# Weight chunks in the order a, a, b, b for the first FFN step, and the last store from another queue

## The chip, the cores and the metric

One core of a Trainium2 chip. The metric is device time in microseconds (us) of one execution; lower is better. Faster or slower needs 2%.

## The reference

A linear attention with decay (4 batches, 8 heads, 768 positions, head size 64) feeds a bilinear FFN on 3072 tokens:

```python
def _attn_ref(q, k, v, lam):            # blocks of 64 positions, cut
    for b in range(nb):
        intra = (qb kb^T * Dmask) vb
        inter = (qb * lam_pow) kv_state
        out = intra + inter
        kv_state = lam_block * kv_state + (kb * rev_pow)^T vb

def _moe_ref(x, w_a, w_b, w_out):       # 512 -> 1536 -> 512
    a = x @ w_a
    b = x @ w_b
    return (a * b @ w_out).astype(np.float32)
```

## The kernel before

The kernel works on 24 blocks of 128 tokens, in groups; TensorE (PE) runs the FFN of one group with the attention of later blocks woven in at "slots". What matters here is the first group, in which the weights are still arriving, and the store of the last rows. SyncE (SP) issues the loads in the order of `pending`; each of the six chunks of `w_a` and of `w_b` (512 KB) is cast to bf16 before use.

```python
W_CHUNKS = (256,) * 6
...
    a_pool = ctx.enter_context(tc.tile_pool(name="a", bufs=3))
...
    pending = []
    for c in range(len(W_CHUNKS)):
        pending += [("a", c), ("b", c)]
...
    def prep_v(u):                       # v of block u to bf16
        make_vb(u, "pool" if u < n0 + 3 else "dve")       # n0 = 4
        pump()
...
    def kv_copy(u, ps, eng="dve"):       # the running state, PSUM to SBUF
        ...
            nc.vector.tensor_mul(st..., ps..., bdiag_bc)
...
    def a_part(f, xT, gt, cuts=None):    # 4 matmuls of 512 columns, copy on ACT
        ps = half(wa_sb, f, xT, gt, "a_ps", cuts)
        a_sb = a_pool.tile([128, 512], BF16, name="a_sb", tag="a")
        nc.scalar.copy(a_sb[:, :gt], ps[:, :gt])
        return a_sb

    def b_part(f, xT, gt, a_sb, ab):     # 4 matmuls, product on DVE
        ps = half(wb_sb, f, xT, gt, "b_ps")
        nc.vector.tensor_mul(ab[:, f, :gt], a_sb[:, :gt], ps[:, :gt])
...
    def store(row, op, lo, hi):
        ...
        o_sb = o_pool.tile([128, d_model], F32, name="o_sb", tag="osb")
        nc.scalar.copy(o_sb[:, lo:hi], op[:, lo:hi])
        nc.sync.dma_start(out=out_r[row][:, lo:hi], in_=o_sb[:, lo:hi])
...
    # ffn(), first group; each chunk holds two f
            for c, w in enumerate(W_CHUNKS):
                fs = range(w_off[c] // 128, w_off[c + 1] // 128)
                a_sbs = [a_part(...) for f in fs]
                if c + 1 < len(W_CHUNKS):
                    cast_w("a", c + 1, "dve")
                for f, a_sb in zip(fs, a_sbs):
                    b_part(f, xT, gt, a_sb, ab)
                    hook(f)              # slot 0: state matmuls of block 3
                if c + 1 < len(W_CHUNKS):
                    cast_w("b", c + 1, "act")
...
    cast_w("a", 0, "pool")               # two instructions of half a chunk
    cast_w("b", 0, "dve")
```

Of the kernel before, what the change touches and what calls it, by code (L numbers as in the profile page):

```python
# [26 lines left out]

GROUPS = (4, 1, 2, 4, 4, 4, 4, 1)
W_CHUNKS = (256,) * 6
W_BUFS = 12  # L30
LOOKAHEAD = (3, 2)
DMA_T_FROM = 9
# [32 lines left out]
def kernel(  # L65
# [11 lines left out]
    nc = tc.nc  # L77
# [4 lines left out]
    d_model, d_ff = moe_w_a.shape  # L82
# [7 lines left out]
    singles = ctx.enter_context(tc.tile_pool(name="singles", bufs=1))  # L90
    wst_pool = ctx.enter_context(tc.tile_pool(name="wst", bufs=W_BUFS))
    ld_pool = ctx.enter_context(tc.tile_pool(name="ld", bufs=4))
# [1 line left out]
    qkT_pool = ctx.enter_context(tc.tile_pool(name="qkT", bufs=5))  # L94
    msk_pool = ctx.enter_context(tc.tile_pool(name="msk", bufs=4))
    xT_pool = ctx.enter_context(tc.tile_pool(name="xT", bufs=2))
    a_pool = ctx.enter_context(tc.tile_pool(name="a", bufs=3))
    ab_pool = ctx.enter_context(tc.tile_pool(name="ab", bufs=2))
    o_pool = ctx.enter_context(tc.tile_pool(name="o", bufs=4))
    ps_pool = ctx.enter_context(tc.tile_pool(name="ps", bufs=1, space=PSUM))  # L100
# [7 lines left out]
    def ps_bank(name, shape, dt, hold=False, ffn=False, at=None):  # L108
        i = bank["next"] if at is None else at
        while i in bank["held"] or (ffn and i == bank["ffn"]):  # L110
            i = (i + 1) % 7
        if ffn:
            bank["ffn"] = i
        bank["next"] = (i + 1) % 7
        if hold:
            bank["held"].add(i)
        return ps_pool.tile(shape, dt, name=name, tag=f"ps{i}")
# [19 lines left out]
    staged = {}  # L137
    w_off = [sum(W_CHUNKS[:i]) for i in range(len(W_CHUNKS) + 1)]

    def load_w(kind, c):  # L140
# [4 lines left out]
        else:  # L145
            w = W_CHUNKS[c]
            t = t[:, :KS * w].rearrange("p (k n) -> p k n", k=KS)
# [4 lines left out]
    def cast_w(kind, c, eng):  # L152
        t = staged.pop((kind, c))
        if kind == "o":
            dst = wo_sb[:, 2 * c:2 * c + 2, :]
        else:
            dst = (wa_sb if kind == "a" else wb_sb)[:, :, w_off[c]:w_off[c + 1]]
        if eng == "act":
            nc.scalar.copy(dst, t)  # L159
        elif eng == "pool":  # L160
            nc.gpsimd.tensor_copy(dst[:, :, :128], t[:, :, :128])
            nc.gpsimd.tensor_copy(dst[:, :, 128:], t[:, :, 128:])
        else:
            nc.vector.tensor_copy(dst, t)  # L164
        pump()

    pending = []
    for c in range(len(W_CHUNKS)):
        pending += [("a", c), ("b", c)]
    n0 = GROUPS[0]  # L170
    pending += [("o", c) for c in range(4)] + [("q", n0), ("k", n0)]
    pending += [("o", 4), ("o", 5), ("v", n0)]
# [4 lines left out]
    def pump():  # L177
        while pending:
            kind, c = pending[0]
            if kind in "abo":  # L180
                if len(staged) >= W_BUFS:
                    return
            elif c >= used["u"] + LOOKAHEAD[used["u"] > 9]:
                return
            pending.pop(0)
            if kind in "abo":
                load_w(kind, c)
            else:
                load_x(kind, c)
# [15 lines left out]
    for w, src in (("q", q), ("k", k)):  # L205
        x4_r = src[0, :, 0:PACK * BLK, :].rearrange("h (p r) d -> p h (r d)", r=PACK)
        for h in range(0, H, 2):
            t = ld_pool.tile([128, H * D], F32, name=w + "4", tag=w + "f")
# [219 lines left out]
    out_r = out.rearrange("(t p) n -> t p n", p=128)  # L428
# [10 lines left out]
    def a_part(f, xT, gt, cuts=None):  # L439
# [5 lines that stand above are left out]
    def b_part(f, xT, gt, a_sb, ab):  # L445
        ps = half(wb_sb, f, xT, gt, "b_ps")
        nc.vector.tensor_mul(ab[:, f, :gt], a_sb[:, :gt], ps[:, :gt])  # L447
# [4 lines left out]
        row, o_sb = kept.pop(0)  # L452
        nc.sync.dma_start(out=out_r[row], in_=o_sb)

    def store(row, op, lo, hi):
        if row < g_u0[KEEP_GROUPS]:
            o_sb = wst_pool.tile([128, 1024], F32, name="o_kept", tag="wst")[:, :d_model]
            nc.scalar.copy(o_sb, op)  # L458
            kept.append((row, o_sb))
            return  # L460
        o_sb = o_pool.tile([128, d_model], F32, name="o_sb", tag="osb")
        nc.scalar.copy(o_sb[:, lo:hi], op[:, lo:hi])  # L462
        nc.sync.dma_start(out=out_r[row][:, lo:hi], in_=o_sb[:, lo:hi])

    def out_mms(op, ab, t, fs, lo=0, hi=d_model):
        for f in fs:
            nc.tensor.matmul(op[:, lo:hi], lhsT=ab[:, f, t * 128:(t + 1) * 128],  # L467
                             rhs=wo_sb[:, f, lo:hi], start=(f == 0), stop=(f == FC - 1))

    def ffn(u0, n, xT, hook, first, last):  # L470
        gt = n * BLK
        ab = ab_pool.tile([128, FC, 512], BF16, name="ab", tag="ab")
        if first:
            for c, w in enumerate(W_CHUNKS):
                fs = range(w_off[c] // 128, w_off[c + 1] // 128)
                a_sbs = [a_part(f, xT, gt, ((0, gt - BLK), (gt - BLK, gt)) if f == 0 else None)
                         for f in fs]
                if c + 1 < len(W_CHUNKS):
                    cast_w("a", c + 1, "dve")
                for f, a_sb in zip(fs, a_sbs):  # L480
                    b_part(f, xT, gt, a_sb, ab)
                    hook(f)
                if c + 1 < len(W_CHUNKS):
                    cast_w("b", c + 1, "act")
            ops = [ps_bank("op", [128, d_model], F32, hold=True) for _ in range(n)]
            slot = FC
            for c in range(FC // 2):
                for t in range(n):
                    out_mms(ops[t], ab, t, range(2 * c, 2 * c + 2))
                    if c == FC // 2 - 1:  # L490
                        store(u0 + t, ops[t], 0, d_model)
                    hook(slot)
                    slot += 1
            bank["held"].clear()
            return
        for f in range(FC):
            a_sb = a_part(f, xT, gt)
            b_part(f, xT, gt, a_sb, ab)
            hook(f)
        for t in range(n):  # L500
            op = ps_bank("op", [128, d_model], F32, ffn=True)
            if last and t == n - 1:
                for lo, hi in ((0, 256), (256, 384), (384, 512)):
                    if lo:
                        op = ps_bank("op", [128, d_model], F32, ffn=True)
                    out_mms(op, ab, t, range(FC), lo, hi)
                    store(u0 + t, op, lo, hi)
                return
            out_mms(op, ab, t, range(FC // 2))
            hook(FC + 2 * t)  # L510
            out_mms(op, ab, t, range(FC // 2, FC))
            store(u0 + t, op, 0, d_model)
            hook(FC + 2 * t + 1)
# [124 lines left out]
    natural_k((3,), (0, 1, 2, 3), 3)  # L638
    cast_w("a", 0, "pool")
    bank["held"].clear()  # L640
    cast_w("b", 0, "dve")
    used["u"] = n0
    pump()

    for g, n in enumerate(GROUPS):
# [6 lines left out]
        def hook(slot, plan=plan):  # L652
            for name, us in plan.get(slot, ()):
                if name == "C":
                    cast_w("o", us, "dve")
                elif name == "PK":
                    prep_k(us)
                elif name == "PV":
                    prep_v(us)
                elif name == "P":  # L660
                    prep_k(us)
                    prep_v(us)
                elif name == "W":
                    store_kept()
                elif name == "T":
                    piece_T(us)
                elif name == "S":
                    piece_S(us)
                elif name == "V":
                    piece_V(us)  # L670
                elif name == "O":
                    pieces_O((us,))
                elif name == "O2":
                    pieces_O(us)
                else:
                    pieces_O(us[:2], us[2:])

        ffn(g_u0[g], n, gx.pop(g), hook, g == 0, g + 1 == len(GROUPS))

# [28 lines left out]
```

## Time and profile before

| | before |
|---|---|
| time, median of 3 | 233.59 us (233.25 to 234.13) |
| span of the profiled execution | 232.6 us |
| PE waits for a weight in the first group | 0.8 us, once |
| first a-matmul of the first chunk / of the third a-chunk | 18.16 / 26.40 us |
| end of the last copy / end of the span | 229.68 / 232.6 us |

The time of a run is some 1.7 us above its span. The profiled execution itself took 234.34 us. PE is busy nearly all the time, so the table names the only two places that the change touches: the first group's weights, and what comes after the last matmul.

### The profile page before, as it was taken

The page shows a single profiled execution, that of the slowest core. Times are in us where ns is not written, and L with a number is a line of the kernel's source. Part 1 is how long each engine was busy: PE and PEld are TensorE (multiplying, and loading weights), DVE is VectorE, ACT ScalarE, POOL GpSimd, SP SyncE. Part 2 cuts the span into 40 slices and gives each one's busy share as a digit, 9 for nine tenths or more (in the row PEclk, how much of TensorE's full clock was granted, in tenths as well). Part 3 has the DMA queues.
Part 4 walks back from the last instruction along what each step waited for, and adds up shares of the span by engine and source line. Part 5 has one row for each costly group of instructions (what it writes and reads, how often), then busy time and mean ns, then how long its engine had stood idle before and what let it go on. Part 6 is the DMA issues. An engine that isn't in the chain of part 4 may idle for free.

```text
span 232.6 us, 4506 instructions
## 1 busy us (share of the span) xinstructions
PE 223.8 (96%) x1756; PEld 124.8 (54%) x1779; DVE 116.4 (50%) x204; ACT 91.0 (39%) x172; POOL 50.4 (22%) x65
## 2 busy tenths in 40 slices
PE   7798999999999999999999999999999999999994
PEld 2574444449698654454544454544454544444493
DVE  1894666646479745684335474235483323332050
ACT  3683764056564342332233332333332333332261
POOL 6061000245655243333300543000300000000000
PEclk9999999999999999999999999999999999999999
DMA  4999999999999999999959997229300220000311
GB/s 150 300 264 351 348 361 298 268 209 193 204 223 164 214 188 221 217 171 205 333 192 206 213 181 129 93 92 202 69 3 0 90 93 0 1 0 10 128 45 48
DMA packets 96453, 38.84 MB, mean 167 GB/s; under 512 B 83376, under 2 KB 91952, under 8 KB 96432
## 3 DMA queue, kind: packets, MB, share of 16 engines
q1 hardware_dynamic: 96288, 38.54, 72.8%
q8 instruction: 14, 0.23, 0.4%
q14 instruction: 7, 0.06, 0.1%
q10 hardware_dynamic: 144, 0.00, 0.0%
HBM read 28.32 MB, written 6.29 MB: 149 GB/s over the span
## 4 chain that ended last, share of the span: by engine, by line
PE 87%; DMA 6%; SPq 3%; ACT 1%; issue 1%; DVE 0%
PE a_ps L434 26%; PE b_ps L434 26%; PE op L467 26%; DMA wst<-in_moe_w_a_dram 4%; SPq L128 3%; PE kq L308 2%; PE o_ps L350 2%; DMA q<-in_q_dram 2%; PE o_ps L340 2%; PE kvd L364 1%; PE tps L294 1%; SPq L149 1%; ACT o_kept L458 1%; DVE wa_sb L164 0%; PE kvd L385 0%
## 5 line engine op out<-in xcount | busy, mean ns | idle before, releaser
L447 DVE TENSOR_TENSOR ab<-a_sb,b_ps 128x512 bf16<-128x512 bf16 (+2 forms) x96 | 52.5, 552 | 76.7 <-PE b_ps L434 55.2
L434 PE MATMUL a_ps<-xT,wa_sb 128*128 128x512 bf16 (+3 forms) x378 | 76.5, 323 | 1.7 <-DVE wa_sb L164 0.8
L434 PE MATMUL b_ps<-xT,wb_sb 128*128 128x512 bf16 (+2 forms) x383 | 77.0, 326 | 0.1
L442 ACT CAST a_sb<-a_ps 128x512 bf16<-128x512 f32 (+2 forms) x96 | 45.5, 481 | 61.5 <-PE a_ps L434 58.1
L467 PE MATMUL op<-wo_sb,ab 128*128 128x512 bf16 (+2 forms) x300 | 64.2, 362 | 0.8 <-issue 0.3
L434 PEld LDWEIGHTS <-wb_sb 128*128 128x128 bf16 x384 | 34.4, 98 | 28.9 <-ACT wb_sb L159 0.5
L434 PEld LDWEIGHTS <-wa_sb 128*128 128x128 bf16 x388 | 33.9, 98 | 29.6 <-DVE wa_sb L164 1.3
L467 PEld LDWEIGHTS <-ab 128*128 128x128 bf16 x312 | 28.8, 98 | 29.9
L325 DVE TENSOR_TENSOR m<-kq,lotri 128x512 bf16<-128x512 f32 x47 | 29.3, 682 | 17.2 <-PE kq L308 17.1
L257 POOL TENSOR_TENSOR qk<-kf,lp_k 128x512 bf16<-128x512 f32 x18 | 19.0, 1056 | 75.1 <-PE a_ps L434 38.1
L262 POOL TENSOR_TENSOR qk<-qf,lp_q 128x512 bf16<-128x512 f32 x20 | 21.8, 1092 | 24.1 <-DMA qf<-in_q_dram 24.1
L462 ACT COPY o_sb<-op 128x512 f32<-128x512 f32 (+2 forms) x19 | 10.3, 541 | 34.0 <-PE op L467 34.0
L357 ACT CAST xT<-o_ps 128x512 bf16<-128x512 f32 x22 | 12.0, 590 | 18.1 <-PE o_ps L350 17.5
L396 DVE TENSOR_TENSOR st<-kvd,bdiag 128x512 bf16<-128x512 f32 x18 | 12.3, 683 | 3.9 <-PE kvd L364 3.2
L271 DVE CAST vb<-vf 128x512 bf16<-128x512 f32 x17 | 9.5, 560 | 0.0
L296 ACT COPY qkT<-tps 128x1024 bf16<-128x1024 bf16 x5 | 5.1, 1012 | 9.9 <-PE tps L294 9.9
L197 PE MATMUL idle<-idle_sb 128*128 128x128 bf16 (+1 forms) x31 | 7.1, 371 | 1.3 <-DVE idle_sb L192 1.3
L350 PE MATMUL o_ps<-m,vb 128*64 128x128 bf16 x192 | 7.9, 222 | 0.0
L271 POOL CAST vb<-vf 128x512 bf16<-128x512 f32 x7 | 4.4, 631 | 13.6 <-DMA vf<-in_v_dram 13.6
L159 ACT CAST wb_sb<-wst 128x1024 bf16<-128x1024 f32 x5 | 5.2, 1046 | 4.7 <-DMA wst<-in_moe_w_b_dram 4.7
L340 PEld LDWEIGHTS <-st 128*128 128x128 bf16 x80 | 5.4, 98 | 2.8
L308 PE MATMUL kq<-qkT 64*128 64x128 bf16 x160 | 6.6, 218 | 0.0
(57 smaller groups left out, 87.4 us busy)
## 6 DMA issues: line engine op xcount, KB each, us to landing
vf<-in_v_dram SPq DMA_DIRECT2D x24, 256.0 KB, 4.9
qf<-in_q_dram SPq DMA_DIRECT2D x20, 256.0 KB, 4.6
kf<-in_k_dram SPq DMA_DIRECT2D x20, 256.0 KB, 4.7
out_dram<-o_sb SPq DMA_DIRECT2D x16, 256.0 KB, 2.0
wst<-in_moe_w_a_dram SPq DMA_DIRECT2D x6, 512.0 KB, 8.8
wst<-in_moe_w_b_dram SPq DMA_DIRECT2D x6, 512.0 KB, 8.8
wst<-in_moe_w_out_dram SPq DMA_DIRECT2D x6, 512.0 KB, 8.6
out_dram<-o_kept SPq DMA_DIRECT2D x7, 256.0 KB, 2.8
```

Source lines behind the costliest of these rows:

```text
L257: eng_of(eng).tensor_mul(qk[:, 1], raw.pop((u, "k")), lp_k[:, u % NB].to_broadcast([128, H, D]))
L262: eng_of(eng).tensor_mul(U[u]["qk"][:, 0], raw.pop((u, "q")), lp_q[:, u % NB].to_broadcast([128, H, D]))
L271: eng_of(eng).tensor_copy(vb, vf)
L308: nc.tensor.matmul(kq[i][:, hp, :], lhsT=d["kT"][p, hp, :], rhs=d["qT"][p, hp, :], start=True, stop=True, skip_group_check=True)
L325: nc.vector.tensor_mul(m, kq[i], lotri_bc)
L350: nc.tensor.matmul(d["o"][p, hp, :], lhsT=d["vb"][:, 2 * hp + i, :], rhs=d["m"](i, hp), start=(first and hp == 0), stop=True, skip_group_c ...
L357: nc.scalar.copy(xT[:, :, col:col + BLK], o_ps)
L396: nc.vector.tensor_mul(st[:].rearrange("p hp i d -> p hp (i d)"), ps[:].rearrange("p hp i d -> p hp (i d)"), bdiag_bc)
L434: nc.tensor.matmul(ps[:, lo:hi], lhsT=w_sb[:, s, f * 128:(f + 1) * 128], rhs=xT[:, s, lo:hi], start=(s == 0), stop=(s == KS - 1), skip_gro ...
L442: nc.scalar.copy(a_sb[:, :gt], ps[:, :gt])
L447: nc.vector.tensor_mul(ab[:, f, :gt], a_sb[:, :gt], ps[:, :gt])
L467: nc.tensor.matmul(op[:, lo:hi], lhsT=ab[:, f, t * 128:(t + 1) * 128], rhs=wo_sb[:, f, lo:hi], start=(f == 0), stop=(f == FC - 1))
```

## The change

The intent: PE does the four a-parts of the first two chunks before it needs any b-weight, so that it has work while b0 travels; and the last store leaves from the queue of the engine that made its data. The diff, less hunks that only carry arguments:

```diff
+W_STEPS = ((0, 1), (2,), (3,), (4,), (5,))
-    a_pool = ctx.enter_context(tc.tile_pool(name="a", bufs=3))
+    a_pool = ctx.enter_context(tc.tile_pool(name="a", bufs=5))
-    for c in range(len(W_CHUNKS)):
-        pending += [("a", c), ("b", c)]
+    for cs in W_STEPS:
+        pending += [("a", c) for c in cs] + [("b", c) for c in cs]
...
-        nc.sync.dma_start(out=out_r[row][:, lo:hi], in_=o_sb[:, lo:hi])
+        (queue or nc.sync).dma_start(out=out_r[row][:, lo:hi], in_=o_sb[:, lo:hi])
...
+            for i, cs in enumerate(W_STEPS):
+                nxt = W_STEPS[i + 1][0] if i + 1 < len(W_STEPS) else None
+                fs = range(w_off[cs[0]] // 128, w_off[cs[-1] + 1] // 128)
...
-                if c + 1 < len(W_CHUNKS):
-                    cast_w("a", c + 1, "dve")
-                for f, a_sb in zip(fs, a_sbs):
+                if i == 0:
+                    cast_w("b", cs[1], "act")
+                elif nxt:
+                    cast_w("a", nxt, "dve")
+                for n_f, (f, a_sb) in enumerate(zip(fs, a_sbs)):
                     b_part(f, xT, gt, a_sb, ab)
                     hook(f)
-                if c + 1 < len(W_CHUNKS):
-                    cast_w("b", c + 1, "act")
+                    if i == 0 and n_f == 1:
+                        cast_w("a", nxt, "dve")
+                if nxt:
+                    cast_w("b", nxt, "act")
...
-                    store(u0 + t, op, lo, hi)
+                    store(u0 + t, op, lo, hi, nc.scalar if hi == d_model else None)
...
     cast_w("a", 0, "pool")
+    cast_w("a", 1, "dve")
     cast_w("b", 0, "dve")
```

More of the change, by code (lines that the diff above doesn't have):

```diff
@@ L453, in store_kept, with store @@
         nc.sync.dma_start(out=out_r[row], in_=o_sb)
-    def store(row, op, lo, hi):
+    def store(row, op, lo, hi, queue=None):
         if row < g_u0[KEEP_GROUPS]:
@@ L473, in ffn @@
         if first:
-            for c, w in enumerate(W_CHUNKS):
-                fs = range(w_off[c] // 128, w_off[c + 1] // 128)
+            for i, cs in enumerate(W_STEPS):
+                nxt = W_STEPS[i + 1][0] if i + 1 < len(W_STEPS) else None
+                fs = range(w_off[cs[0]] // 128, w_off[cs[-1] + 1] // 128)
                 a_sbs = [a_part(f, xT, gt, ((0, gt - BLK), (gt - BLK, gt)) if f == 0 else None)
                          for f in fs]
-                if c + 1 < len(W_CHUNKS):
-                    cast_w("a", c + 1, "dve")
-                for f, a_sb in zip(fs, a_sbs):
+                if i == 0:
[3 more added lines that the diff above has]
+                for n_f, (f, a_sb) in enumerate(zip(fs, a_sbs)):
                     b_part(f, xT, gt, a_sb, ab)
                     hook(f)
-                if c + 1 < len(W_CHUNKS):
-                    cast_w("b", c + 1, "act")
+                    if i == 0 and n_f == 1:
+                        cast_w("a", nxt, "dve")
+                if nxt:
+                    cast_w("b", nxt, "act")
             ops = [ps_bank("op", [128, d_model], F32, hold=True) for _ in range(n)]
```

## The prediction

> **What bounds the kernel now.** I began with the page of the run before, parts 1 and 2: who is busy, and at what clock.
>
> ```profile
> span 232.6 us, 4506 instructions
> PE 223.8 (96%) x1756; PEld 124.8 (54%) x1779; DVE 116.4 (50%) x204; ACT 91.0 (39%) x172; POOL 50.4 (22%) x65
> ...
> PE   7798999999999999999999999999999999999994
> ...
> PEclk9999999999999999999999999999999999999999
> ```
>
> TensorE (PE) is busy 96% of the span at full clock; what is not full lies in the first 20 us and in the last slice. From about 25 us to the end the kernel is one stream of matmuls, so a change of order can only gain what PE idles near the start, plus something after the last matmul. The change touches exactly these two places. It adds and removes no arithmetic: in the two builds every engine has the same instructions, except that one store moves from SyncE's (SP's) queue to ScalarE's (ACT's).
>
> Next I asked what PE waits for, longest first:
>
> ```profile
> PE idle L197 <- DVE idle_sb L192: 1.3, 1, 1.3
> PE tk L541 <- DVE scratch L532: 1.0, 2, 0.8
> PE a_ps L434 <- DVE wa_sb L164: 0.8, 1, 0.8
> ```
>
> The third line is the one in reach: the first a-part of weight chunk 1 waits once, 0.8 us, for VectorE's (DVE's) cast of that chunk to bf16. The chain that ended last, between 13 and 30 us, says what stands behind that cast:
>
> ```profile
> 13.54 8.48 DMA wst<-in_moe_w_a_dram
> 22.02 0.02 issue
> 22.05 0.70 DVE wa_sb L164
> 22.75 0.05 issue
> 22.80 1.90 PE a_ps L434 x8
> 24.70 1.87 PE b_ps L434 x8
> ```
>
> A transfer of 8.5 us, a cast, then nothing but PE. I name the 512 KB chunks a0, b0, a1, b1, a2 in their old order of issue. The timelines of DVE and of ACT show arrivals as the moment an idle caster is released by a DMA (columns: start, duration, instruction, idle time before it and what ended it); first DVE, whole from 19 to 26 us, then one line of ACT:
>
> ```profile
> 19.12 0.69 DVE L164 CAST wb_sb<-wst 128x1024 bf16<-128x1024 f32 x1 [0.68 <-DMA wst<-in_moe_w_b_dram]
> 22.05 0.69 DVE L164 CAST wa_sb<-wst 128x1024 bf16<-128x1024 f32 x1 [2.23 <-DMA wst<-in_moe_w_a_dram]
> 22.66 0.68 DVE L447 TENSOR_TENSOR ab<-a_sb,b_ps 128x512 bf16<-128x512 bf16 x1
> 23.25 0.68 DVE L396 TENSOR_TENSOR st<-kvd,bdiag 128x512 bf16<-128x512 f32 x1
> 23.85 0.68 DVE L447 TENSOR_TENSOR ab<-a_sb,b_ps 128x512 bf16<-128x512 bf16 x1
> 25.06 0.69 DVE L164 CAST wa_sb<-wst 128x1024 bf16<-128x1024 f32 x1 [0.53 <-DMA wst<-in_moe_w_a_dram]
> ```
>
> ```profile
> 23.56 1.04 ACT L159 CAST wb_sb<-wst 128x1024 bf16<-128x1024 f32 x1 [2.88 <-DMA wst<-in_moe_w_b_dram]
> ```
>
> Chunks land at 17.2 (GpSimd, released for a0's cast), 19.1, 22.05, 23.56 and 25.06 us. The third comes 2.9 us after the second, and then one comes every 1.5 us, while PE uses one in 1.73 us. So the third arrival is the last one that PE really waits for: 22.05 plus 0.70 for its cast, and PE starts at 22.80, whatever it did before.
>
> **What the Trainium skill says.** "DMA: Bandwidth & Descriptors", section "Queues, rings and completion order", says that SP and ACT each own one ring on each of the same 16 DMA engines and that an engine takes descriptors in ring order. So arrivals should go by place in SP's queue, not by which weight a chunk holds. The trace agrees as far as it goes: from the third on, a- and b-chunks land alternately at equal steps of 1.5 us. The same page, section "Issuing engines are not separate DMA queues", says that issuing from several engines only saves sequencer time. In the trace SP is not short of it at the end: its last wait is for ACT's copy. "TensorE: Matmul & The Clock Gate", section "Wait — 56ns, not 53.3ns?", gives 215.7 ns for a warm 512-column matmul; eight in 1.73 us (216 ns) agree, so I use 0.216 us.
>
> **The front, part by part.** The new order of chunks is a0, a1, b0, b1, then as before. Since all four have one size and one access pattern, I keep the arrival times by place: a1 gets 19.1 and b0 gets 22.05.
>
> PE does a0 from 18.16 to about 19.9 in both kernels. Now a1 is cast at 19.12 to 19.81, so PE does its eight a-matmuls at about 19.86 to 21.6. Before, b0 ran in that slot, with the four small state matmuls of block 3 between its halves (begun at 20.76, the next b-matmul at 20.98: 0.22 us). Those matmuls hang on the first b-part, so they move behind the wait. The new wait is for b0: landed 22.05, cast to 22.75, first b-matmul 22.80. It is the same instant as before. The PE wait named above gets longer, from 0.8 to about 1.1 us, and its releaser changes from wa_sb to wb_sb.
>
> After 22.80 the old kernel had 16 large matmuls to do before a2: 16 x 0.216 = 3.46 us, plus 0.13 us lost waiting for ACT's cast of b1 (1.86 us instead of 1.73 between the first a- and the first b-matmul); a2 starts at 26.40. The new one has the same 16 plus the state matmuls: 3.46 + 0.22 = 3.68 us. b1's cast is over at 24.60 in either (ACT's copies of the four a-parts are done by then), and the new b1 starts at 22.80 + 1.73 + 0.22 = 24.75, so the 0.13 us disappear. PE is ready for a2 at 26.48: **0.09 us later** than before.
>
> Does a2's cast hold it up? DVE takes it after two products and the state copy. The first product needs the b-half plus the 0.28 us that the trace shows between the nominal end of a half and the next product (25.80 against 24.66 + 0.86): 22.80 + 0.86 + 0.28 = 23.94. Successive DVE instructions of this size start 0.60 us apart (22.66, 23.25, 23.85), so state copy 24.54, second product 25.14, a2's cast 25.74 to 26.43, PE from 26.48. It just fits, with no margin; at worst, if the starts come 0.69 us apart, 0.25 us more. From a2 on, arrivals stay ahead of PE, and the order is the old one. A shift at this place should reach the end, as PE has no slack.
>
> The larger pool of a-tiles (5 instead of 3) only makes room for four held parts.
>
> **The end.** I read the last line of ACT's and of SP's timeline, and SP's waits in the last 19 us:
>
> ```profile
> 229.41 0.27 ACT L462 COPY o_sb<-op 128x128 f32<-128x128 f32 x1 [0.40 <-PE op L467]
> ...
> 228.47 1.56 SPq L463 DMA_DIRECT2D out_dram<-o_sb  x3
> ...
> SPq L703 <- DMA out_dram<-o_sb: 1.3, 1, 1.3
> ```
>
> The last copy ends at 229.68; the last of SP's three issues ends at 228.47 + 1.56 = 230.03, and an issue takes 0.33, so it starts at 229.70. Only about 0.02 us lie between copy and issue, so SP is waiting for ACT, not catching up. On ACT's queue this handover between engines can at best vanish. The landing (1.6 us for a 64 KB store) and the closing after it (232.6 - 231.3 = 1.3 us) stay. I put **-0.02 us**.
>
> The sum: +0.09 - 0.02 = +0.07 us, or nothing measurable: the three runs before spread over 0.9 us.
>
> **Rivals.** (1) The intended gain: four a-parts in a row give PE work while the b-chunks travel, and the 0.8 us wait goes. It would need the third chunk to land about 1 us earlier than now. For it: the 2.9 us gap is odd beside the later 1.5, so it may be accidental. Against it: a chunk is a chunk, and the queue moves 340 to 365 GB/s through this stretch. Time 232.8. (2) The arrivals of the first four shift the other way, as two neighbouring pieces of the same matrix are now in flight together; nothing in the profile speaks for or against, and 0.5 us later gives 234.1. (3) DVE becomes the bound of this step, as a2's cast stands behind more: +0.25, so 233.9. (4) ACT's queue is slow for a lone store: its only other transfer, lam, took 3.5 us for 4 KB, but at the cold start and as a load of tiny pieces. If the store took 0.5 us longer, 234.1. (5) In runs without the profiler the chunks land earlier and neither order waits: no change.
>
> **Range and chances.** My working says 233.59 + 0.07 = 233.66; rival 1 seems a little more likely than 2 to 4 together in its sign, so I go to 233.6. The spread before (233.25 to 234.13) and the rivals (232.8 to 234.1) give 232.9 to 234.3 for 8 in 10. A 2% change is 4.7 us, over five times all PE idle in reach: same 0.98, 0.01 each side.
>
> **What would show it.** Right: the third weight chunk still lands at about 22 us and is now b's; PE's wait is on wb_sb, 1.0 to 1.2 us; the first a-matmul of a2 starts at 26.4 to 26.7; the store on ACT's queue starts within 0.05 us of the copy and lands in about 1.6 us. Wrong: the third arrival moves by over 0.5 us, or PE waits again after 25 us for a cast of a2, or the closing after the last copy (2.9 us, 229.68 to 232.6) changes by more than 0.2 us.

## The result, and the profile after

| | before | after |
|---|---|---|
| time, median of 5 each | 233.81 us (233.25 to 234.29) | 233.96 us (233.89 to 234.54) |
| ratio, 95% interval | | 1.0011 (0.9989 to 1.0033) |
| span of the profiled execution | 232.6 us | 232.2 us |

No difference in time.

The total was as predicted, the way to it was not. The page of the kernel after, then PE's waits in it, longest first:

```profile
span 232.2 us, 4527 instructions
PE 225.0 (97%) x1779; PEld 124.5 (54%) x1779; DVE 115.7 (50%) x204; ACT 91.2 (39%) x172; POOL 50.0 (22%) x65
```

```profile
PE tq L547 <- DVE scratch L538: 1.0, 3, 0.4
PE a_ps L435 <- POOL wa_sb L162: 0.6, 1, 0.6
...
PE o_ps L341 <- DVE st L397: 0.2, 1, 0.2
```

I had forecast a wait of PE for wb_sb of 1.0 to 1.2 us. There is none. PE waits instead for GpSimd's cast of the very first chunk, a0, and there is a new short wait for DVE's copy of a state (st). The 23 matmuls more in the second page are records missing in the first; both builds have the same ones. The chain that ended last, from 11 to 27 us:

```profile
11.72 6.09 DMA wst<-in_moe_w_a_dram
17.81 0.05 issue
17.86 0.62 POOL wa_sb L162
18.49 0.05 issue
18.53 3.64 PE a_ps L435 x20
22.17 0.86 PE b_ps L435 x4
23.03 0.22 PE kvd L365 x4
23.26 2.59 PE b_ps L435 x12
```

Once a0 is there, PE runs through all four chunks: the a-parts, the b-parts, and between them the state matmuls (kvd), now behind the first b-part as predicted. DVE's timeline shows why b0 is not waited for:

```profile
19.33 0.69 DVE L165 CAST wa_sb<-wst 128x1024 bf16<-128x1024 f32 x1 [0.88 <-DMA wst<-in_moe_w_a_dram]
20.84 0.69 DVE L165 CAST wb_sb<-wst 128x1024 bf16<-128x1024 f32 x1 [0.81 <-DMA wst<-in_moe_w_b_dram]
```

The third chunk landed at 20.84 us, not at 22.05, and its cast was done before PE had finished the a-parts. The first a-matmul of the third a-chunk, a2, starts at 25.78 us, 0.62 us earlier than in the kernel before. Yet the last copy ends only 0.19 us earlier (229.49 against 229.68). I laid PE's attention matmuls of the two traces side by side: every one from 46 to 80 us is 0.60 or 0.61 us early, every one from 83 us on 0.19 us. So 0.42 us are lost in one place, at 82 us. DVE there in the kernel after, then GpSimd, then PE:

```profile
80.08 1.09 DVE L272 CAST vb<-vf 128x512 bf16<-128x512 f32 x1
81.09 0.68 DVE L397 TENSOR_TENSOR st<-kvd,bdiag 128x512 bf16<-128x512 f32 x1
...
79.84 1.04 POOL L258 TENSOR_TENSOR qk<-kf,lp_k 128x512 bf16<-128x512 f32 x1 [4.14 <-PE op L468]
...
81.82 0.40 PE L341 MATMUL o_ps<-qkT,st 128*128 128x128 bf16 x4 [0.24 <-DVE st L397]
```

and the same instructions of DVE and GpSimd in the kernel before:

```profile
80.69 0.67 DVE L271 CAST vb<-vf 128x512 bf16<-128x512 f32 x1
81.28 0.68 DVE L396 TENSOR_TENSOR st<-kvd,bdiag 128x512 bf16<-128x512 f32 x1
...
80.03 1.04 POOL L257 TENSOR_TENSOR qk<-kf,lp_k 128x512 bf16<-128x512 f32 x1 [4.14 <-DMA kf<-in_k_dram]
```

The same cast of v takes 1.09 us in one and 0.67 in the other; the shortest of its kind in either trace take 0.41 to 0.42 us. In each case it ends 0.29 us after GpSimd's instruction does (80.08 + 1.09 = 81.17 against 79.84 + 1.04 = 80.88; 81.36 against 81.07). The Trainium skill, "SBUF — State Buffer", section "Who interferes with whom", says that DVE and GpSimd share one pair of ports under an exclusive lock, that casts can take it, and that whoever starts second "fully blocks". The traces agree. The cast came 0.61 us earlier with PE, GpSimd's instruction only 0.19 us (79.84 against 80.03), so the cast now met its first quarter instead of its last third. What sets GpSimd's time is not shown. A second execution of the unchanged kernel before (before_again, below) shows how far it wanders:

```profile
78.23 1.04 POOL L257 TENSOR_TENSOR qk<-kf,lp_k 128x512 bf16<-128x512 f32 x1 [4.77 <-PE kq L308]
```

That is 1.8 us earlier for the same instruction, while PE's matmuls there were 0.2 us earlier. Whether the two meet is thus a matter of the execution at least as much as of the change.

Two theories then. **A**: when a weight chunk lands varies from execution to execution, whatever the order; front gains or losses travel to the end unless a v cast on DVE collides with GpSimd; on average the change is worth nothing. **B**: the new order itself brings the third chunk 1.2 us earlier and wins 0.6 us at the front, which the collision regularly eats.

### The profile page after: what moved, and what is told of

It reads as the page before. It is cut to its first block, busy times and chain, and to the rows that moved or that the text cites. A ratio compares the mean times of both kernels' runs of the same rounds, so it can differ in the third digit from the quotient of the medians.

```text
span 232.2 us, 4527 instructions
## 1 busy us (share of the span) xinstructions
PE 225.0 (97%) x1779; PEld 124.5 (54%) x1779; DVE 115.7 (50%) x204; ACT 91.2 (39%) x172; POOL 50.0 (22%) x65
## 4 chain that ended last, share of the span: by engine, by line
PE 88%; DMA 5%; SPq 3%; DVE 1%; ACT 1%; issue 0%; POOL 0%; DVEq 0%
PE a_ps L435 27%; PE b_ps L435 27%; PE op L468 25%; DMA wst<-in_moe_w_a_dram 3%; PE kq L309 2%; SPq L129 2%; PE o_ps L351 2%; DMA q<-in_q_dram 2%; PE o_ps L341 2%; PE kvd L365 1%; PE tps L295 1%; DVE m L326 1%; ACT o_kept L459 1%; DVE st L397 0%; POOL wa_sb L162 0%
## 5 line engine op out<-in xcount | busy, mean ns | idle before, releaser
L468 PE MATMUL op<-wo_sb,ab 128*128 128x512 bf16 (+2 forms) x312 | 65.6, 363 | 0.0
L198 PE MATMUL idle<-idle_sb 128*128 128x128 bf16 (+1 forms) x31 | 6.6, 349 | 1.3 <-DVE idle_sb L193 1.3
L351 PEld LDWEIGHTS <-vb 128*64 128x64 bf16 x192 | 5.8, 109 | 1.5 <-POOL vb L272 0.2
```

The costliest lines, as they stand in the source:

```text
L351: nc.tensor.matmul(d["o"][p, hp, :], lhsT=d["vb"][:, 2 * hp + i, :], rhs=d["m"](i, hp), start=(first and hp == 0), stop=True, skip_group_c ...
L468: nc.tensor.matmul(op[:, lo:hi], lhsT=ab[:, f, t * 128:(t + 1) * 128], rhs=wo_sb[:, f, lo:hi], start=(f == 0), stop=(f == FC - 1))
```

## The experiments

Twelve runs (nine new kernels and three repeats), five timed rounds each; all gave correct results. The table holds one profiled execution of each, and of the two kernels from above. "a0 PE" is the start of PE's first a-matmul, "a2" the start of the first a-matmul of the third a-chunk, "stretch" from a2 to the end of the last copy, "closing" from there to the end of the span (good to 0.05 us, as the span is rounded). The third arrival is the start of DVE's cast; DVE was idle before it in all fourteen, until the load landed.

| kernel | loads, steps | cast of a0 | third arrival | a0 PE | a2 | a0 to a2 | stretch | closing |
|---|---|---|---|---|---|---|---|---|
| before | old | 17.20 | 22.05 | 18.16 | 26.40 | 8.24 | 203.28 | 2.92 |
| before_again | old | 17.25 | 21.38 | 18.28 | 26.04 | 7.76 | 203.44 | 2.92 |
| store_only | old | 17.44 | 20.90 | 18.11 | 25.26 | 7.15 | 204.08 | 2.76 |
| old_store_vb | old | 17.34 | 21.80 | 18.40 | 26.46 | 8.06 | 203.26 | 2.78 |
| old_vb | old | 17.14 | 20.51 | 18.13 | 25.27 | 7.14 | 203.26 | 2.77 |
| after | new | 17.86 | 20.84 | 18.53 | 25.78 | 7.25 | 203.71 | 2.71 |
| after_again | new | 17.61 | 20.97 | 18.28 | 25.53 | 7.25 | 203.29 | 2.78 |
| order_only | new | 18.84 | 21.82 | 19.51 | 26.76 | 7.25 | 203.29 | 2.95 |
| last2_act | new | 18.71 | 21.69 | 19.39 | 26.63 | 7.24 | 203.36 | 2.71 |
| vb_act | new | 17.65 | 20.93 | 18.32 | 25.57 | 7.25 | 203.27 | 2.76 |
| vb_act_again | new | 18.16 | 21.14 | 18.83 | 26.08 | 7.25 | 203.27 | 2.75 |
| vb_act_a2 | new, a2 cast sooner | 17.59 | 21.03 | 18.26 | 25.47 | 7.21 | 203.26 | 2.77 |
| a0_early | new, a0 before last v | 17.21 | 20.98 | 18.74 | 25.97 | 7.23 | 203.30 | 2.73 |
| late_a1 | old loads, new steps | 18.44 | 21.41 | 19.11 | 27.68 | 8.57 | 203.29 | 2.73 |

### The two kernels again, and each half of the change alone

before_again and after_again have no edit. order_only is the change with `store(u0 + t, op, lo, hi)` put back; store_only is the kernel before with

```diff
-                    store(u0 + t, op, lo, hi)
+                    store(u0 + t, op, lo, hi, nc.scalar if hi == d_model else None)
```

> The kernel before against itself, to learn how far one build varies. Theory A (arrival of the third weight chunk is an accident of each execution, the same for both orders): the ratio's interval covers 1, and the profiled third arrival may lie anywhere from 20.8 to 22.1 us. Theory B (the new order of loads is what brings the third chunk 1.2 us earlier): the profile shows it again at 22.05 within 0.3 us.

> The changed kernel once more. Theory A (accident): the third arrival need not be at 20.8 us again. Theory B (the order): 20.8 us within 0.3. Both: ratio 0.998 to 1.004, and if the front is again early by 0.6 us, PE loses about 0.4 us of it near 82 us, behind VectorE's cast of v for block 11.

> The new order without the store on ACT's queue. If the order decides the small difference: within 0.1 us of the changed kernel. Closing after the last copy: 2.9 us as in the kernel before under the theory that ACT's queue shortens it (2.9 to 2.7 in the one trace), 2.7 us if that difference is chance.

> The old order with the last store on ACT's queue. My prediction: ratio 1.000, gain at most 0.02 us. Rival: the closing after the last copy gets 0.2 us shorter (2.7 instead of 2.9), ratio 0.999. The third arrival tells as for the kernel before: B says 22.05, A says anything.

Measured against the kernel before (median 234.12 in these rounds): before_again 234.27, ratio 1.0017 (0.9988 to 1.0045); after_again 233.81, 0.9993 (0.9967 to 1.0019); order_only 234.12, 1.0002 (0.9976 to 1.0029); store_only 233.77, 0.9995 (0.9967 to 1.0022). One kernel against itself differs as much as any of them, so that order_only would lie within 0.1 us of the changed kernel can't be told (it lay 0.31 us from after_again).

B falls: with the old loads the third chunk landed at 20.51 to 22.05 us in five traces, with the new ones at 20.84 to 21.82 in seven. store_only has the old order and no wait for weights at all. Nor was the collision regular, as I had half expected: after_again had the early front and lost nothing (its v cast took 0.42 us). store_only lost the most, 0.80 us, nearly all of it at 74 us, one block earlier. DVE's cast, GpSimd's instruction beside it, and PE's wait in store_only:

```profile
72.39 1.18 DVE L271 CAST vb<-vf 128x512 bf16<-128x512 f32 x1
...
72.24 1.04 POOL L262 TENSOR_TENSOR qk<-qf,lp_q 128x512 bf16<-128x512 f32 x1
...
74.55 0.38 PE L364 MATMUL kvd<-vb,qk 128*128 128x128 bf16 x4 [0.63 <-DVE st L396]
```

72.39 + 1.18 = 73.57, again 0.29 us after GpSimd's 73.28.

### The place in the queue

late_a1: the changed kernel with the old order of loads, so that the second chunk it needs comes third.

```diff
-    for cs in W_STEPS:
-        pending += [("a", c) for c in cs] + [("b", c) for c in cs]
+    for c in range(len(W_CHUNKS)):
+        pending += [("a", c), ("b", c)]
```

> The changed kernel, but SP loads a0, b0, a1, b1 in the old order, so the second a-chunk it needs is the third to arrive. If arrival goes by place in the queue: a1 lands 1.5 to 2.9 us later than in the changed kernel, PE waits for its cast, and the front is 0.9 to 2.3 us later, ratio to the kernel before 1.004 to 1.010. If arrival does not matter: ratio 1.000.

Measured: 235.06 us against 233.98, ratio 1.0039 (1.0024 to 1.0054), the one kernel clearly slower than the one before, by a little less than the 1.004 to 1.010 expected. PE's two waits for weights, and the second of them on PE's timeline:

```profile
PE a_ps L435 <- DVE wa_sb L165: 1.1, 1, 1.1
PE a_ps L435 <- POOL wa_sb L162: 1.1, 1, 1.1
...
22.17 1.90 PE L435 MATMUL a_ps<-xT,wa_sb 128*128 128x512 bf16 x8 [1.14 <-DVE wa_sb L165]
```

So arrival goes by place in SP's queue and matters when the chunk is needed: 8.57 us from a0 to a2 instead of 7.25. This step of the prediction holds.

### The casts of v on another engine

vb_act: the changed kernel with the casts for blocks 10 and 11, the two that were met, on ACT.

```diff
-        make_vb(u, "pool" if u < n0 + 3 else "dve")
+        make_vb(u, "pool" if u < n0 + 3 else "act" if u in (10, 11) else "dve")
```

vb_act_again is the same file; old_store_vb is store_only with this line; old_vb is the kernel before with nothing else.

> The changed kernel with the casts of v for blocks 10 and 11 on ACT instead of DVE. Theory: what is gained or lost at the front reaches the end unless one of these two DVE casts runs beside a GpSimd instruction (0.42 us alone, 0.7 to 1.2 beside one) and PE then waits for the state copy near 74 or 81 us. Then in this kernel no such wait is left, from the first a-matmul of a2 to the end of the last copy it takes 203.3 us in any execution, and the mean time falls by 0.1 to 0.5 us against the changed kernel (ratio to before about 0.998). Rival: DVE's queue there is not the cause; a wait of PE for the state copy remains, or ACT's products of the step come late instead and the time stays or rises.

> The new order, the store on ACT and the two v casts on ACT, once more. Theory: ratio to the kernel before 0.9965 to 0.999, 203.28 us (within 0.03) from the first a-matmul of a2 to the end of the last copy. If its first result was luck of arrivals: ratio 1.000.

> The old order with the store and the two v casts on ACT. Theory (the order itself is worth nothing on average): same as vb_act_again within 0.3 us. Rival (the new order gains at the front, and only the later stall hid it): this kernel is 0.3 to 0.6 us slower than vb_act_again. Stretch from a2 to the last copy 203.28 us also here.

> The kernel before with nothing but the two v casts on ACT. Theory: 0.15 to 0.2 us slower than old_store_vb (the closing), and up to 0.3 us faster than the kernel before (the stalls near 74 and 81 us that go), ratio 0.9985 to 1.000; stretch 203.28 us, closing 2.9 us.

Measured: vb_act 233.42 against 233.98, ratio 0.9978 (0.9962 to 0.9994); in other rounds, against 233.76: vb_act_again 233.62, 0.9993 (0.9972 to 1.0013); old_store_vb 233.39, 0.9985 (0.9962 to 1.0008); old_vb 233.20, 0.9980 (0.9959 to 1.0001). In all these traces, and in vb_act_a2, the stretch is 203.26 or 203.27 us whatever the front was (a2 from 25.27 to 26.46), while three of nine traces with the casts on DVE lost 0.16 (before_again), 0.42 (after) and 0.80 us (store_only). last2_act's 203.36 is another matter: its last copy starts 0.07 us later after the copy before it. In vb_act the state copy near 80 us has no cast before it any more:

```profile
79.87 0.69 DVE L397 TENSOR_TENSOR st<-kvd,bdiag 128x512 bf16<-128x512 f32 x1
80.48 0.42 DVE L272 CAST vb<-vf 128x512 bf16<-128x512 f32 x1
```

This shows the cause of the losses. By count alone, none of five against three of nine, it would be weak; but each loss sits at one place, at a state copy that stood behind a stretched cast, and before_again's 0.16 us is what its cast took above 0.42 (0.58 us, ending 0.29 us after GpSimd's instruction again). The gain in time is small: the three losses make 0.15 us a kernel over those nine traces, and the ratios, 0.0018 below 1 on average over the four and vb_act_a2 (0.4 us), are only partly clear of noise. vb_act_again's ratio missed the expected 0.9965 to 0.999. The old order with this line is no slower than the new one: the rival that the new order wins at the front is not supported. old_vb was to be 0.15 to 0.2 us slower than old_store_vb; it was not, so that expectation failed.

### The last two stores

last2_act: as the change, with `nc.scalar if lo else None` for `nc.scalar if hi == d_model else None`.

> The changed kernel with the last two stores on ACT's queue. If the closing gets shorter because SP has no store of its own in flight at the end, the closing after the last copy (2.92, 2.92, 2.95 with SP, 2.71, 2.78, 2.76 with ACT so far) is 2.7 or a little less. If it was chance it is anywhere from 2.7 to 2.95.

Measured: 234.08, ratio 1.0004 (0.9986 to 1.0021); closing 2.71 us. The end in the kernel after: ACT's queue, then SP's last wait.

```profile
229.51 0.35 ACTq L464 DMA_DIRECT2D out_dram<-o_sb  x1
...
SPq L710 <- DMA out_dram<-o_sb: 2.0, 1, 2.0
```

The copy ended at 229.49: the handover takes 0.02 us as before, and the store lands in 1.6 us as before. What differs lies behind the landing. Over all traces the closing is 2.71 to 2.78 us in ten of ten with ACT's queue, and 2.92, 2.92, 2.95 and 2.77 with SP's. In the three long ones SP's last instruction of the kind DRAIN takes 0.12 to 0.13 us, and 0.007 us in all others. So ACT's queue goes with 0.15 to 0.2 us less, but old_vb shows that SP's queue can end as quickly; what decides it stays open, and no timed ratio resolves it.

### The first chunk earlier

a0_early: one load moved ahead of the fourth v.

```diff
     for u in range(n0):
+        if u == n0 - 1:
+            load_w(*pending.pop(0))
         load_x("v", u)
```

> The changed kernel with the load of a0 ahead of the fourth v-load. In all three traces of the new order PE waits for GpSimd's cast of a0 (0.6, 0.4, 1.5 us) and for no weight after it. Theory (the first chunk's arrival bounds the front of the new order): that wait goes, a2 starts at 25.3 to 25.6, 0.2 to 0.6 us gained on average. Rival: the fourth v comes later in exchange, or the next chunks are then waited for, and nothing is gained.

Measured: 234.19, ratio 1.0012 (0.9986 to 1.0038). The wait for a0 goes, as expected, but PE waits 0.8 us for GpSimd's cast of the fourth v, and begins a0 at 18.74. So a2 starts at 25.97 us and not at the expected 25.3 to 25.6: the rival was right, the fourth v came later in exchange.

### The cast of a2 sooner

vb_act_a2: vb_act with `if i == 0 and n_f == 0:` for `n_f == 1`.

> As vb_act, with DVE's cast of a2 one product earlier. In every trace of the new order it takes 7.25 us from the first a-matmul of a0 to the first of a2, 0.1 us more than the 7.15 us of the one trace of the old order without a wait for weights, and PE starts a2 0.05 us after that cast ends. If the place of the cast is the cause: 7.15 us here, and 0.1 us less time than vb_act_again (not clear of noise); otherwise 7.25.

Measured: 233.30 against 233.76, ratio 0.9976 (0.9958 to 0.9995). a0 to a2 took 7.21 us, between the two expected values. From the first b-matmul to a2 it is 3.69 us (21.78 to 25.47) against 3.77 or 3.78 in every other trace of the new steps, so the wait for a2's cast is gone; another 0.05 us came in before b0, whose cast ended at 21.72. Its median is the lowest of the new order here, 0.46 us below the kernel before in its rounds: far from 2%, with the interval clear of 1, but not to be told from vb_act (0.9978) or from old_vb, which has the old order and in the same rounds the lower median (233.20).

## Why the prediction was right

- **The total.** 233.96 us lies in the range, and "same" was right. All repeats agree. The way to it was partly luck: in the two profiled executions the front came 0.62 us earlier, 0.42 us of that was lost at 82 us, and the closing was 0.2 us shorter, where +0.09 and -0.02 had been summed. By its own list the working was wrong: the third arrival moved by 1.21 us, more than the 0.5 named there, and the change of the closing (0.21 us, as rounded) is at its limit of 0.2.
- **Arrival by place: right as a rule, wrong as a number.** I kept "the arrival times by place", with 22.05 us for the third, out of one execution. That was the latest of the fourteen. The step that failed is therefore "The new wait is for b0": no trace with the new loads has such a wait of more than 0.05 us. In the old order the same spread gave waits of 0 to 0.8 us in the five traces. Rival 1 was closer here: the old wait does go. The a0-to-a2 time is 7.24 us on average over the seven traces with the new loads (vb_act_a2 among them, a0_early and late_a1 not), against 7.67 over the five of the old order.
- **Not because PE has more to do.** Here is when PE first needs the second and the third chunk in a trace without a wait of the old order (store_only), then a0 and the third chunk in the new order (after):

```profile
18.11 1.91 PE L434 MATMUL a_ps<-xT,wa_sb 128*128 128x384 bf16 x11 [0.27 <-POOL wa_sb L161]
19.85 1.03 PE L434 MATMUL b_ps<-xT,wb_sb 128*128 128x512 bf16 x4
...
21.80 1.89 PE L434 MATMUL a_ps<-xT,wa_sb 128*128 128x512 bf16 x8
```

```profile
18.53 3.64 PE L435 MATMUL a_ps<-xT,wa_sb 128*128 128x384 bf16 x20 [0.59 <-POOL wa_sb L162]
22.01 1.03 PE L435 MATMUL b_ps<-xT,wb_sb 128*128 128x512 bf16 x4
```

The old order needs the second chunk 1.74 us after a0 and the third 3.69 us after it; the new one needs the second after the same eight matmuls (an estimate from the first fence: 1.74 us) and the third after 3.48 us, sooner, as the state matmuls moved behind. So the intent, work for PE while b0 travels, is not met: b0 moves one place back in the queue together with its use, and no place in the queue is needed later than before. What differs is when a0 lands.
- **Where that 0.43 us went.** PE starts a0 at 18.73 us on average in those seven and at 18.22 in the five: 0.51 us later, since a0 lands later (cast at 17.6 to 18.8 us against 17.1 to 17.4). a2 starts at 25.97 and 25.89 on average, 0.09 us apart. In the seven, b0's cast ends only 0.06 to 0.48 us before PE uses it; had a0 come 0.51 us earlier and b0 not, all seven would have waited for b0 (an estimate). Why a0 lands later is open. It fits rival 2 of the prediction, two pieces of one matrix in flight together, but late_a1 has the old order of loads and a0 at 18.44, so the order of loads alone is not the reason.
- **The 0.09 us.** I had summed it from state matmuls that move behind the wait (+0.22) and a cast of b1 no longer waited for (-0.13). Neither counts when the third chunk is in time: then the old order takes 7.14 or 7.15 us, state matmuls included, and the new one 7.25. That 0.1 us is DVE's cast of a2, the one I had called just in time "with no margin". That the two sizes agree is luck.
- **"A shift at this place should reach the end, as PE has no slack."** It did in six of nine traces with the v casts on DVE. In three it shrank at 74 or 81 us, where a state copy stood behind a v cast that met GpSimd; which of the two moved there differs from execution to execution. I had listed DVE only for the first group.
- **The store.** The -0.02 us did not come: copy to issue takes 0.02 us on ACT's queue too (229.49 to 229.51). (The line that the prediction shows for SP's last wait is that for the landing; the wait for ACT's copy is the one before.) The 0.15 to 0.2 us behind the landing I had not seen, so the sign is right for another reason, and the size is below what the times can tell.

## What to carry to other kernels

An arrival read from one trace is one draw: before reasoning from a wait of under 1 us in a start-up phase, profile the same kernel two or three times (the third chunk of the kernel before came at 22.05 and at 21.38 us). Then ask how long after its first matmul PE needs each chunk: an order that leaves these times as they are has nothing to gain there. When an early gain does not reach the end, lay the two traces side by side by matching instructions; here the offset stayed within 0.01 us (0.60 or 0.61) until the place where it broke, and that place named the second wait. In this kernel two short DVE casts stood before something that PE waits for, where a GpSimd instruction may run; ACT took them at no cost that a trace shows.

## What the Trainium skill lacked or had wrong

- "SBUF — State Buffer", section "Who interferes with whom": the lock is described, and the runs agree, but the section gives no time for a cast that meets it: a 128x512 f32 to bf16 cast took 0.42 us alone and 0.67, 1.09 and 1.18 us when it began inside a GpSimd multiply of 1.04 us, ending 0.29 us after the multiply each time.
- "DMA: Bandwidth & Descriptors", section "Issuing engines are not separate DMA queues": it names only sequencer time as what another queue saves. The closing of the program after the last copy was 2.71 to 2.78 us in ten traces with the last store on ACT's queue, and 2.92 to 2.95 in three of four with SP's (2.77 in the fourth). Whether the queue is the cause is open.
- No page that I read says how much the landing of one load varies between executions: the third weight chunk landed at 22.05 and 21.38 us in two executions of the kernel before, and at 20.51 to 22.05 us over the five traces with the old kernel's loads and steps.
